# Storing the filter's spectrum during the weave of filter and first input, with e table 0 and fillers moved

## The chip, the cores and the metric

The kernel runs on one core of a Trainium2 chip: TensorE (PE, with its weight loads listed as PEld), VectorE (DVE), ScalarE (ACT), GpSimd (POOL) and SyncE (SP, which issues DMAs only). The metric is the device time of one execution in microseconds (us). Before the change the median of three runs is 2032.61 us (2030.9 to 2034.29).

## The reference

Two computations follow each other. The first is a long convolution of x (8 batches, 5696 positions, 128 channels) with a filter h, by Fourier transforms of length 11392; the second mixes its result over positions with two 5696x5696 matrices.

```python
Xf = np.fft.rfft(x, n=2 * S, axis=1)
Hf = np.fft.rfft(h, n=2 * S, axis=0)
y = np.fft.irfft(Xf * Hf[None], n=2 * S, axis=1)[:, :S]

theta = y @ w_theta
zr, zi = y * np.cos(theta), y * np.sin(theta)
m = einsum('ts,bsd->btd', w_tok_r, zr) + einsum('ts,bsd->btd', w_tok_i, zi)
u = y + m
out = u + np.maximum(u @ w_ch, 0.0)
```

## The kernel before

**Tiling of the convolution.** The transform of length 11392 is split into 178 x 64. The work is cut into eight groups, each two batches and one half (64) of the channels. A group has four stages. Stage A (`stage_a`, L242) multiplies by the first transform `f1_t`: 16 blocks of four matmuls, each block into one PSUM tile, which DVE (L258) or ACT (L260) copies into the tile `a`. The second transform (`f2`, L263) reads all of `a` and makes 12 blocks of 8 frequencies (the last has 2). In stage B (`stage_b`, L415) ACT copies each such block out of PSUM (`xs`, L435), and DVE multiplies it by the filter's spectrum into `uv_t` (L437 or, for group 0, L442). Stage C (`stage_c`, L448) needs all of `uv_t`: 16 blocks of 16 matmuls, copied out by DVE (L464) or ACT (L462) into `g`. Stage D multiplies by the `e` tables (`e_t`) and writes the result out. The program weaves the stages: stage C of a group with stage A of the next, then stage B of the next with stage D of the group.

**The filter first.** h goes through stage A and `f2` like an input. `h_chunk` (L360) does one block of its spectrum: `f2`, and a copy with a scale back into the place of h's own stage-A tile (`a_h`; a__240 in the profile), on DVE for five of the blocks (L365), on ACT for the others (L367). The 12 calls of `h_chunk` are woven with the 16 stage-A blocks of the first input x0 (`a0`, by the list `A_WITH`). This is called the weave here. Inside x0's blocks stand fillers, matmuls whose result nobody reads (`idle`, L237); the argument `spare` of `stage_a` says how many and how wide. The last third of the table `w_t2`, the small tables `r_u` and `r_v` and the start of `e` table 0 are made in the weave or right after it.

**Where the spectrum goes.** Group 0 takes it from `a_h` directly: the product needs the rows also swapped by 64, and for these two SP DMAs a block copy them into one of four `hs` tiles (L425). Four blocks' copies are issued by `load0`, and each block's step issues those of the fourth block after it. All later groups read the spectrum from HBM (`hf_hbm`, L427). Twelve SP DMAs store it there (`h_store`, L371 to L375), four for blocks 0 to 5, four for 6 to 10 and four for block 11; six more, from HBM to HBM, add the swapped rows (`swap_rows`, L405 to L410). Stage A of group 1 (`a__1406`) uses the buffer of `a_h`, so its first copy waits until all that reads `a_h` is done.

**What sets the order.** Up to the end of group 0's stage C, DVE, ACT and POOL run in the order in which the program is written (`manual_schedule`). PE and SP are ordered by a planner over the whole kernel, by priority and by its own estimates, with waits on semaphores; `issue_after` puts what stands in its block behind a given instruction on that instruction's engine. After group 0's stage C the planner orders all engines, apart from two stretches of the mixing in which DVE is fixed again.

**e tables.** `e_table(n)` (L393) gives four steps: the nearest whole turn (two DVE instructions, L399 and L400), the absolute value (DVE, L198), the sine (ACT, L195) and the cosine (ACT, L202), each over 90x979 elements. Tables 1 and 2 and the negatives (`e_minus`) are made in group 0's stage C. All three are first used in its stage D.

Of the kernel before, what the change touches and what calls it, by code (L numbers as in the profile page):

```python
# [22 lines left out]
def kernel(  # L23
# [10 lines left out]
    nc = tc.nc  # L34
# [44 lines left out]
    K1 = N1 // 2 + 1  # L79
# [8 lines left out]
    NCK = len(CHK)  # L88
# [15 lines left out]
    def psum():  # L104
        return fp.tile([P, 2, 512], F32, tag="ps", name="ps")
# [20 lines left out]
    a_0 = s1.tile([P, 2 * K1, HD], F16, name="a_0")  # L126
# [67 lines left out]
    def sine(out_, r, sign):  # L194
        nc.scalar.activation(out_, r, AF.Sin, bias=zero_b[:r.shape[0]], scale=-sign * TWO_PI)  # L195

    def absolute(k, r):
        nc.vector.tensor_scalar(k.bitcast(mybir.dt.uint32), r.bitcast(mybir.dt.uint32), 0x7FFFFFFF, None,  # L198
                                op0=ALU.bitwise_and)

    def cosine(out_, k):
        nc.scalar.activation(out_, k, AF.Sin, bias=half_pi[:k.shape[0]], scale=-TWO_PI)  # L202
# [6 lines left out]
    w_t2 = keep.tile([P, K1, 3 * N2], F16, tag="keep", name="w_t2")  # L209
# [27 lines left out]
    def idle(ps, n, of, m):  # L237

        for i in range(n):
            nc.tensor.matmul(ps[:, i % 2, 512 - m:], of[:, :P], of[:, P:P + m], start=True, stop=True)  # L240
# [83 lines left out]
    pad = v_t[:, 5 * D * CK:6 * D * CK]  # L324
# [20 lines left out]
    for n, f in enumerate(steps):  # L345
# [5 lines left out]
            w_rest(1)  # L351
        f()
    w2_absolute()

    def hst_of(c, n=1):
        c0 = CHK[c][0]
        c1 = CHK[c + n - 1][0] + CHK[c + n - 1][1]
        return a_h["a"].rearrange("p (h k) d -> p h (k d)", h=2)[:, :, c0 * HD:c1 * HD]

    def h_chunk(c):  # L360
        c0, ck = CHK[c]
        ps = f2(a_h, c, 0)
        dst = hst_of(c).rearrange("p h (d k) -> p h d k", k=ck)
        if c in (0, 2, 5, 7, 10):
            nc.vector.tensor_scalar(dst, ps, 16.0 / NF, None, op0=mult)  # L365
        else:
            nc.scalar.activation(dst, ps, AF.Copy, scale=16.0 / NF)  # L367
        for cc, j in ((0, 0), (NCK - 1, CHK[-1][1] - 1)):
            if c == cc:
                nc.vector.tensor_scalar(dst[:, :, :, j], dst[:, :, :, j], 0.5, None, op0=mult)  # L370
    def h_store(i):  # L371
        i, h, ri = i // 4, i // 2 % 2, i % 2
        c0, c1, w = ((0, NCK // 2, HD * CK), (NCK // 2, NCK - 1, HD * CK), (NCK - 1, NCK, HD * CHK[-1][1]))[i]
        nc.sync.dma_start(hf_hbm[c0:c1, h, :64, ri, :w].rearrange("c p n -> p c n"),
                          hst_of(c0, c1 - c0)[64 * ri:64 * ri + 64, h].rearrange("p (c n) -> p c n", n=w))  # L375
# [17 lines left out]
    def e_table(n):  # L393

        n0 = 11 * n
        t, k, r = ((e_y[0], e_f[1], e_y[0]), (e_y[1], e_y[0], e_y[1]), (e_f[2], e_y[1], e_y[0]))[n]

        def nearest():
            nc.vector.tensor_scalar(k, t, MAGIC, None, op0=add)  # L399
            nc.vector.scalar_tensor_tensor(r, k, MAGIC, t, op0=ALU.subtract, op1=ALU.subtract)  # L400
        t3, k3 = (z.rearrange("p (n m) -> p n m", m=NB) for z in (r, k))
        return (nearest, lambda: absolute(k, r), lambda: sine(e_t[:K1, n0:n0 + 11, 1, :], t3, -1),
                lambda: cosine(e_t[:K1, n0:n0 + 11, 0, :], k3))

    def swap_rows():  # L405
        for c0, c1, w in ((0, NCK // 2, HD * CK), (NCK // 2, NCK - 1, HD * CK), (NCK - 1, NCK, HD * CHK[-1][1])):
            for ri in range(2):
                dst, src = (hf_hbm[c0:c1, :, r0:r0 + 64, r, :w].rearrange("c h p n -> (c h) p n")
                            for r0, r in ((64, ri), (0, 1 - ri)))
                nc.sync.dma_start(dst, src)  # L410

    def e_minus():
        nc.vector.tensor_scalar(e_neg[:K1], e_t[:K1, 1:2 * NP:2], -1.0, None, op0=mult)

    def stage_b(a_st, dh, warm=WARM, first=False):  # L415

        hs_of = {}

        def load(c):
            if c >= NCK:  # L420
                return
            hs = hs_of[c] = fh.tile([P, 2, HD * CK], F16, tag="hs", name="hs")
            w = HD * CHK[c][1]
            for e in range(2 if first else 0):
                nc.sync.dma_start(hs[64 * e:64 * e + 64, 1, :w], hst_of(c)[64 - 64 * e:128 - 64 * e, dh])  # L425
            if not first:
                nc.sync.dma_start(hs[:, :, :w], hf_hbm[c, dh, :, :, :w])  # L427

        def chunk(c):
            c0, ck = CHK[c]  # L430
            hv = hs_of[c][:, :, :HD * ck].rearrange("p r (d k) -> p r d k", k=ck)
            straight = hst_of(c)[:, dh].rearrange("p (d k) -> p d k", k=ck).unsqueeze(1) if first else hv[:, 0:1]
            ps = f2(a_st, c, warm)
            xs = fs.tile([P, 2, HD, CK], F16, tag="xs", name="xs")
            nc.scalar.activation(xs[:, :, :, :ck], ps, AF.Copy)  # L435
            if ck == CK and not first:
                nc.vector.tensor_tensor(  # L437
                    uv[:, :, :, c0:c0 + ck],
                    xs.rearrange("p e d k -> p e (d k)").unsqueeze(1).to_broadcast([P, 2, 2, HD * CK]),
                    hv.rearrange("p r d k -> p r (d k)").unsqueeze(2).to_broadcast([P, 2, 2, HD * CK]), op=mult)  # L440
            for r in range(2 if ck < CK or first else 0):
                nc.vector.tensor_tensor(  # L442
                    uv[:, 2 * r:2 * r + 2, :, c0:c0 + ck], xs[:, :, :, :ck],
                    (hv[:, 1:2] if r else straight).to_broadcast([P, 2, HD, ck]), op=mult)
            load(c + LEAD)
        return [lambda c=c: load(c) for c in range(LEAD)], [lambda c=c: chunk(c) for c in range(NCK)]

    def stage_c(st, last):  # L448
# [65 lines left out]
    def front(g, by_dve=(), a_=None, spare=None):  # L514
        if g >= len(groups):
            return [], [], []
        bp, dh = groups[g]
        x16 = x16s[g].rearrange("p b n d -> p (b n) d")
        steps, a_st = stage_a(lambda q: x16[:NB, :, q], by_dve, a_, spare)
        return (steps, *stage_b(a_st, dh, 0 if g else WARM // 2, g == 0))  # L520

    A_WITH = (1, 1, 1, 2, 1, 2, 1, 2, 1, 2, 2)
    a0, load0, b0 = front(0, (1, 3, 5, 8, 11, 13), a_0, (1, w_t2[:, 2:5].rearrange("p k n -> p (k n)"), 512 - 4 * K1))
    rr = []
    r_rest = [lambda: rr.extend([r_table(0, r_u), r_table(1, r_v)]), lambda: rr[0](), lambda: rr[1]()]
    e0 = e_table(0)
    h_chunk(0)
    w2_sine()
    for c in range(1, NCK):
        if c == 5:  # L530
            w_rest(2)
        h_chunk(c)
        if c == 1:
            w2_cosine()
        for _ in range(min(len(a0), A_WITH[c - 1])):
            a0.pop(0)()
        if c in (8, 9, 10):
            r_rest.pop(0)()
    for f in load0:
        f()  # L540
    for f in e0[:2]:
        f()
    for f in a0:
        f()
    fronts = {1: front(1)}
    for n, f in enumerate(b0):
        f()
        h_store(n)
        if n in (3, 6):
            e0[n // 3 + 1]()  # L550
        if n % 2:
            idle(psum(), 1, w_t2[:, 2:6].rearrange("p k n -> p (k n)"), 512)
    idle(psum(), 6, w_t2[:, 2:6].rearrange("p k n -> p (k n)"), 512)
# [232 lines left out]
    for g, (bp, dh) in enumerate(groups):  # L786
        st = {}
        last = g + 1 == len(groups)
        a_, load_, b_ = fronts.pop(g + 1) if g + 1 in fronts else front(g + 1)
        if last:  # L790
            for _ in range(3):
                steps0.pop(0)()
        now = ([with_load(steps0.pop(0), n < 6) for n in range(9)] if last else [], 0.0, 0.88)
        c_ = stage_c(st, last)
        if g == 0:
            swap_rows()
            now = ([*e_table(1), *e_table(2), e_minus], -0.06, 0.62)
        woven((c_, 0.06 if a_ else 0.0, 1.0), (a_, 0.0, 0.88), now, load_, (load_x(g + 2, st), 0.1, 1.02))
        if g == 0:
            ordered.close()  # L800
        if g + 2 == len(groups):
            xin.close()
            open_phases()
            load_ya0()
        now = [steps0.pop(0) for _ in range(4)] if last else []
        woven((b_, 0.0, 0.8), (stage_d(st, bp, dh, load_ya1 if last else None, g + 2 == len(groups)), 0.08 if b_ else 0.0, 1.1 if b_ else 1.0), now)
        if g + 2 == len(groups):
            load_ya1(st["yt"], True)
            open_ring()
# [333 lines left out]
    for i, (k, p, tt, j0, s0, nj) in enumerate(stretches):  # L1143
# [47 lines left out]
        if tt is None:  # L1191
# [21 lines left out]
            if end_of_pair:  # L1213
# [5 lines left out]
                c, c0 = c_last  # L1219
# [183 lines left out]
```

## Time and profile before

| | |
|---|---|
| median of three runs | 2032.61 us |
| the profiled execution | 2031.42 us, span 2029.6 us |
| PE busy | 1944.0 us (96% of the span) |
| DVE, ACT, POOL busy | 1538.6, 636.1, 976.0 us |
| the weave: first matmul of h's second transform to the first of x0's | 25.09 to 47.84 us |
| group 0's product, up to the first long run of stage C | 47.84 to 67.16 us |
| group 0's stage C, up to its last copy | 67.16 to 93.4 us |
| group 1's stages A and C (for comparison) | 115.0 to 132.5 us |

A row of an engine's sequence shows the start, the time from there to the end of the last of the merged instructions, the engine, the line, the operation, what it writes and reads, the shape and the count; in brackets stands the engine's idle time before it and what ended it. A matmul's row includes its way through the array, so in a row of matmuls the distance of the starts tells the cost of one. A row of the table by stretches shows, for each engine, busy time and instructions, and at the end the clock that TensorE was granted (1.00 is full), a DMA share and the GB/s moved.

### The profile page before, as it was taken

What the parts mean: (1) busy time and instruction counts of PE and PEld (TensorE: products, weight loads), DVE (VectorE), ACT (ScalarE), POOL (GpSimd) and SP (SyncE); (2) the same over time, 40 slices, a digit from 0 to 9 for tenths busy, and PEclk for the clock granted to TensorE, in tenths of its full rate; (3) what the DMA queues carried; (4) which work ended last, traced back from release to release, by engine and by line L of the source; (5) the groups of instructions that cost most, each with busy time, mean ns of one, the idle gap of its engine ahead of it and who ended that gap; (6) DMA issues with size and microseconds to landing.
All of it is one profiled execution on the core that took longest, in us unless ns stands there. A gap on an engine that the chain in (4) does not pass through costs nothing.

```text
span 2029.6 us, 42459 instructions
## 1 busy us (share of the span) xinstructions
PE 1944.0 (96%) x16124; PEld 1077.7 (53%) x16300; DVE 1538.6 (76%) x2819; ACT 636.1 (31%) x934; POOL 976.0 (48%) x1787
## 2 busy tenths in 40 slices
PE   7789898889999999999999998999999999999998
PEld 6688888644444444444444444444444444444444
DVE  7777887766778787887877668768677776777767
ACT  6778887852232323232300000011111111111111
POOL 8333413584453635454566454554535445354450
PEclk8999999999999999999999999999999999999999
DMA  9999997999798989999999799896978879798793
GB/s 130 161 159 175 159 173 211 257 238 189 150 183 171 180 168 162 181 174 179 167 171 152 121 255 217 132 153 123 153 131 149 148 129 154 126 155 139 135 156 85
DMA packets 508525, 332.48 MB, mean 164 GB/s; under 512 B 186727, under 2 KB 461671, under 8 KB 508231
## 3 DMA queue, kind: packets, MB, share of 16 engines
q0 software_dynamic: 322656, 157.47, 61.1%
q1 hardware_dynamic: 177792, 159.17, 27.0%
q10 hardware_dynamic: 7872, 13.11, 1.9%
q8 instruction: 128, 2.10, 0.4%
q14 instruction: 77, 0.63, 0.1%
HBM read 373.24 MB, written 92.95 MB: 230 GB/s over the span
## 4 chain that ended last, share of the span: by engine, by line
PE 40%; DMA 4%; DVE 3%; POOL 2%; issue 2%; ACT 0%; DVEq 0%; POOLq 0%; ACTq 0%
PE m L1338 37%; POOL ring L687 2%; DMA ring<-in_moe_w_tok_i_dram 2%; DVE c L1345 1%; PE v L998 1%; PE utp L991 1%; PE m L1342 1%; DMA ring<-in_moe_w_tok_r_dram 1%; DVE wt L911 1%; DMA wl<-in_moe_w_tok_i_dram 0%; DVE b L848 0%; DMA cp_hbm<-c 0%; DMA wl<-in_moe_w_tok_r_dram 0%; PE m L1206 0%; DMA c<-cp_hbm 0%
## 5 line engine op out<-in xcount | busy, mean ns | idle before, releaser
L687 POOL DMA_DIRECT2D ring<-in_moe_w_tok_i_dram x720 | 388.7, 546 | 660.9 <-DVE wt L911 576.5
L911 DVE STREAM_TRANSPOSE wt<-ring 128x384 f32<-128x384 f32 (+2 forms) x720 | 359.6, 524 | 116.7 <-PE m L1338 74.9
L687 POOL DMA_DIRECT2D ring<-in_moe_w_tok_r_dram x720 | 387.3, 546 | 126.1 <-DVE wt L911 71.5
L1338 PE MATMUL m<-b,wt 128*128 128x512 bf16 x1600 | 382.7, 379 | 3.8 <-DVE wt L911 1.7
L1338 PEld LDWEIGHTS <-wt 128*128 128x128 bf16 x1804 | 176.0, 98 | 215.5 <-DVE wt L911 4.3
L1345 DVE TENSOR_TENSOR c<-c,m 128x512 f32<-128x512 f32 x412 | 266.1, 671 | 0.4 <-PE m L1338 0.4
L993 ACT ACTIVATE ring<-utp 128x512 bf16<-128x512 bf16 x85 | 50.7, 597 | 571.6 <-PE utp L991 571.6
L457 PE MATMUL ps<-r_u,uv_t 128*128 128x128 f16 x1024 | 118.8, 222 | 7.4 <-DVE g__1420 L464 3.7
L458 PE MATMUL ps<-r_v,uv_t 128*128 128x100 f16 x1024 | 116.8, 210 | 1.1 <-DVE uv_t L442 1.1
L988 ACT ACTIVATE ub<-c 128x512 bf16<-128x512 f32 x88 | 55.2, 628 | 199.3 <-DMA ring<-in_moe_w_tok_i_dram 116.9
L1239 PE MATMUL m<-b,wt 128*128 128x512 bf16 x471 | 111.4, 382 | 6.3 <-issue 3.0
L153 POOL DMA_DIRECT2D x<-in_x_dram x128 | 97.5, 767 | 23.8 <-POOL x L151 14.8
L458 PEld LDWEIGHTS <-uv_t 128*128 128x128 f16 x1024 | 101.5, 99 | 9.9 <-issue 7.4
L437 DVE TENSOR_TENSOR uv_t<-xs,hs 128x2048 f16<-128x2048 f16 x77 | 91.4, 1223 | 16.2 <-ACT xs L435 9.0
L457 PEld LDWEIGHTS <-uv_t 128*128 128x128 f16 x1024 | 101.6, 99 | 1.2 <-DVE uv_t L442 1.0
L435 ACT ACTIVATE xs<-ps 128x1024 f16<-128x1024 f32 x96 | 90.5, 972 | 25.9 <-PE ps L271 12.2
L1239 PEld LDWEIGHTS <-wt 128*128 128x128 bf16 x528 | 50.4, 98 | 64.7 <-issue 7.8
L573 ACT ACTIVATE red<-theta_ps,magic 128x512 f32<-128x512 f32 (+1 forms) x46 | 31.6, 687 | 153.5 <-PE theta_ps L571 96.3
L271 PEld LDWEIGHTS <-w_t 64*128 64x128 f16 x3240 | 57.9, 99 | 25.6 <-issue 20.7
L941 ACT ACTIVATE ring<-tpz 128x512 bf16<-128x512 bf16 (+1 forms) x46 | 27.5, 597 | 136.6 <-PE tpz L939 123.0
L251 PE MATMUL ps<-f_t,x 89*128 89x180 f16 x512 | 65.2, 258 | 1.9 <-DVE a__240 L365 1.1
L1000 DVE SCALAR_TENSOR_TENSOR c<-v,c 128x512 f32<-128x512 f32 x88 | 60.1, 684 | 2.8 <-PE v L998 2.1
(2932 smaller groups left out, 3737.2 us busy)
## 6 DMA issues: line engine op xcount, KB each, us to landing
ring<-in_moe_w_tok_r_dram POOLq DMA_DIRECT2D x352, 96.0 KB, 4.4
ring<-in_moe_w_tok_i_dram POOLq DMA_DIRECT2D x352, 96.0 KB, 4.9
ring<-in_moe_w_tok_r_dram POOLq DMA_DIRECT2D x352, 80.0 KB, 4.4
ring<-in_moe_w_tok_i_dram POOLq DMA_DIRECT2D x352, 80.0 KB, 3.9
cp_hbm<-c SPq DMA_DIRECT2D x88, 256.0 KB, 2.5
c<-cp_hbm SPq DMA_DIRECT2D x88, 256.0 KB, 4.3
out_dram<-c SPq DMA_DIRECT2D x88, 256.0 KB, 4.4
hs<-hf_hbm SPq DMA_DIRECT2D x77, 256.0 KB, 3.6
```

The source lines that it names most:

```text
L153: nc.gpsimd.dma_start(x16[p0:p1, e, n0:n0 + 16, :HD], bass.AP(tensor=src.tensor, offset=src.offset + (p0 * N2 + n0) * D + dh * HD, ap=[[N2 ...
L251: nc.tensor.matmul(ps[:, i // 2, (i % 2) * 2 * K1:(i % 2 + 1) * 2 * K1], lhs(q + i), f1_t[:NB], start=True, stop=True)
L435: nc.scalar.activation(xs[:, :, :, :ck], ps, AF.Copy)
L437: nc.vector.tensor_tensor(uv[:, :, :, c0:c0 + ck], xs.rearrange("p e d k -> p e (d k)").unsqueeze(1).to_broadcast([P, 2, 2, HD * CK]), hv. ...
L457: nc.tensor.matmul(o, u_t[:, at:at + P], r_u, start=True, stop=False)
L458: nc.tensor.matmul(o[:, 2 * NP:], v_t[:, at:at + P], r_v, start=False, stop=True)
L687: nc.gpsimd.dma_start(wb[32 * i:32 * i + 32, :ng, :nj * 64], bass.AP(tensor=a.tensor, offset=a.offset + row0 * S + p * H + i * QR + j0 * 6 ...
L911: nc.vector.transpose(wt.rearrange("p j t r -> p (j t r)").bitcast(F32).rearrange("p (j g t) -> p g j t", j=TJ, g=4)[:, :ng, :nj], wb[:, : ...
L1000: nc.vector.scalar_tensor_tensor(c[:m], v[:m], 0.0, c[:m], op0=ALU.max, op1=ALU.add)
L1239: nc.tensor.matmul(ms[n // 2 * 2 + h], a[n][:, j, :, r], bts_of[p][jj][n % 2 * 2 + h][:, r, :], start=(n % 2 == 0 and jj == 0 and r == 0), ...
L1338: nc.tensor.matmul(ms[q], a[q][:, j, :, r], bts[jj][q][:, r, :], start=(jj == 0 and r == 0), stop=(jj == NJ - 1 and r == 1 and q not in left))
L1345: nc.vector.tensor_tensor(c, z, ms[q], op=op)
```

## The change

Six things are edited, all ahead of the end of group 0's stage C.

1. Five fillers of 512 columns over the tile `pad` are put behind h's stage A and ahead of the first `h_chunk`.
2. The fillers inside x0's stage-A blocks go (one of 152 columns in each, now none).
3. Other blocks are given to DVE: of the spectrum 0, 2, 6, 8, 10 instead of 0, 2, 5, 7, 10; of x0's stage A 1, 3, 7, 9, 12, 14 instead of 1, 3, 5, 8, 11, 13.
4. The steps of the r tables follow blocks 9, 10 and 11 instead of 8, 9 and 10, and with them go the nearest turn, the absolute value and the sine of e table 0; its cosine follows the weave. Before, the DVE steps followed the weave, and the sine and the cosine followed blocks 3 and 6 of group 0's product.
5. The stores: four behind block 6 of the weave, four behind block 10, the last four behind block 0 of group 0's product. Before, one stood behind each of the product's twelve blocks.
6. The six DMAs of the swapped rows are put, on SP, behind the last copy into `hs` of group 0.

```diff
@@ -351,6 +351,7 @@
     w2_absolute()
+    idle(psum(), 5, pad, 512)
@@ -361,7 +362,7 @@
-        if c in (0, 2, 5, 7, 10):
+        if c in (0, 2, 6, 8, 10):
             nc.vector.tensor_scalar(dst, ps, 16.0 / NF, None, op0=mult)
@@ -412,6 +413,8 @@
+    last_hs = []
+
     def stage_b(a_st, dh, warm=WARM, first=False):
@@ -422,7 +425,7 @@
             for e in range(2 if first else 0):
-                nc.sync.dma_start(hs[64 * e:64 * e + 64, 1, :w], hst_of(c)[64 - 64 * e:128 - 64 * e, dh])
+                last_hs.append(nc.sync.dma_start(hs[64 * e:64 * e + 64, 1, :w], hst_of(c)[64 - 64 * e:128 - 64 * e, dh]))
@@ -520,10 +523,10 @@
-    a0, load0, b0 = front(0, (1, 3, 5, 8, 11, 13), a_0, (1, w_t2[:, 2:5].rearrange("p k n -> p (k n)"), 512 - 4 * K1))
+    a0, load0, b0 = front(0, (1, 3, 7, 9, 12, 14), a_0, (0, w_t2[:, 2:5].rearrange("p k n -> p (k n)"), 512 - 4 * K1))
...
-    e0 = e_table(0)
+    e0 = list(e_table(0))
@@ -534,20 +537,20 @@
         for _ in range(min(len(a0), A_WITH[c - 1])):
             a0.pop(0)()
-        if c in (8, 9, 10):
+        if c >= NCK - 3:
             r_rest.pop(0)()
-    for f in load0:
-        f()
-    for f in e0[:2]:
-        f()
-    for f in a0:
+            e0.pop(0)()
+        if c in (NCK // 2, NCK - 2):
+            for n in range(4):
+                h_store(n + (0 if c == NCK // 2 else 4))
+    for f in load0 + a0 + e0:
         f()
     fronts = {1: front(1)}
     for n, f in enumerate(b0):
         f()
-        h_store(n)
-        if n in (3, 6):
-            e0[n // 3 + 1]()
+        if n == 0:
+            for i in range(8, 12):
+                h_store(i)
@@ -793,7 +796,8 @@
         if g == 0:
-            swap_rows()
+            with tc.issue_after(last_hs[-1].ins):
+                swap_rows()
             now = ([*e_table(1), *e_table(2), e_minus], -0.06, 0.62)
```

## The prediction

> **What bounds the kernel now.** I read the page first (busy shares, the slices), then the stages by stretches of time, then each engine's own sequence of instructions at the two places that the change touches. From the page, the busy shares and the granted clock in 40 slices of about 51 us:
>
> ```profile
> PE 1944.0 (96%) x16124; PEld 1077.7 (53%) x16300; DVE 1538.6 (76%) x2819; ACT 636.1 (31%) x934; POOL 976.0 (48%) x1787
> PE   7789898889999999999999998999999999999998
> PEclk8999999999999999999999999999999999999999
> ```
>
> TensorE bounds the whole, but the first two slices are the emptiest, and the clock is below full in the first. All that is edited runs between 23 and 93 us; what comes later only starts earlier or later. Next the same stretch, cut where the granted clock changes (busy us of each engine, then clock, DMA share, GB/s):
>
> ```profile
> 21.97:25.38 3.41, 2.04 (x39) 1.84 (x39) 3.01 (x5) 3.41 (x6) 3.30 (x9) 1.00 1.13 68
> 25.38:28.79 3.41, 3.41 (x95) 2.97 (x88) 1.95 (x3) 2.56 (x4) 3.30 (x8) 0.50 0.02 5
> ...
> 32.20:35.62 3.42, 2.20 (x63) 1.96 (x55) 3.31 (x5) 2.60 (x4) 3.33 (x5) 1.00 1.61 160
> 35.62:39.03 3.41, 3.21 (x73) 2.59 (x72) 2.28 (x3) 0.77 (x1) 3.27 (x4) 0.50 1.94 209
> 39.03:42.44 3.41, 3.41 (x51) 2.80 (x52) 1.31 (x5) 3.40 (x6) 3.41 (x6) 0.50 1.40 215
> 42.44:45.86 3.42, 3.42 (x55) 2.98 (x55) 3.34 (x7) 1.57 (x3) 1.73 (x4) 0.50 2.40 145
> ...
> 66.30:69.73 3.43, 0.92 (x15) 0.81 (x16) 2.95 (x5) 0.00 (x0) 0.00 (x0) 1.00 0.59 113
> 69.73:73.15 3.42, 2.39 (x24) 2.38 (x24) 1.65 (x2) 2.57 (x4) 1.73 (x3) 0.50 0.54 157
> 73.15:76.56 3.41, 3.41 (x36) 3.41 (x35) 0.55 (x1) 3.41 (x5) 0.18 (x1) 0.50 1.04 282
> ```
>
> See that three stretches with a TensorE pause (2.04, 2.20 and 0.92 us busy) are each followed by half clock. After the second the clock stays at 0.50 up to 52.7 us, and there TensorE is full while DVE and ACT wait for it. Last, the sequences of PE, ACT, DVE and SP where group 0 passes from the product with the spectrum to stage C:
>
> ```profile
> 35.29 0.49 PE L251 MATMUL ps<-f_t,x 89*128 89x180 f16 x4 [1.14 <-DVE a__240 L365]
> ...
> 70.76 0.27 PE L457 MATMUL ps<-r_u,uv_t 128*128 128x128 f16 x1 [2.69 <-DVE g__1420 L464]
> ...
> 70.58 0.77 ACT L260 ACTIVATE a__1406<-ps 128x720 f16<-128x720 f32 x1 [6.13 <-DMA hf_hbm<-hf_hbm]
> ...
> 66.71 0.39 DVE L442 TENSOR_TENSOR uv_t<-xs,hs 128x256 f16<-128x256 f16 x1 [1.26 <-DMA hs<-a__240]
> ...
> 65.26 3.70 SPq L374 DMA_DIRECT2D hf_hbm<-a__240  x5
> 69.01 2.78 SPq L410 DMA_DIRECT2D hf_hbm<-hf_hbm  x3
> ```
>
> ACT stands still for 6.13 us. The row names the swap, but the tile that ACT is to write (a__1406) takes the place of the spectrum's tile (a__240), and what still reads a__240 then are the five stores of 65.26 to 68.96; with their fastest landing of 1.8 us the last ends at 70.2 to 70.7, where ACT starts. Meanwhile three PSUM buffers of four hold x1's stage-A blocks that ACT should empty, so TensorE pauses 2.69 us and falls to half clock.
>
> **The change part by part.** Three stretches carry it: the weave (25.09 to 47.84, 22.75 us), group 0's product (47.84 to 67.16, 19.3 us) and group 0's stage C (67.16 to 93.4, 26.2 us).
>
> *Fillers ahead of the weave.* Five 128x512 matmuls; seven such in a row at full clock take 1.80 us, so five about 1.2 us. TensorE idles 1.28 us before 25.09 (it waits for ACT's last copy of stage A), so they lie in that pause; late by the wait for a PSUM buffer they cost 0 to 0.3 us. They fill the stretch that preceded the first fall of the clock.
>
> *Fillers inside x0's stage A go.* Sixteen 128x152 matmuls, 0.13 us apart at half clock (45.92 to 46.05) and 0.07 at full: 1.1 to 2.1 us of TensorE, on the path where the clock is half.
>
> *DVE and ACT in the weave.* The change of who empties which block moves no total: 5 spectrum blocks and 6 stage-A blocks stay on DVE, 7 and 10 on ACT. e table 0 comes in: on DVE 0.66+1.17+0.67 = 2.5 us, on ACT 1.10+1.11 = 2.2 us. Needs then: DVE 5x1.22 + 6x0.90 + 0.85 (halved bins) + 1.68 (the last third of w) + 2.4 (r tables) + 0.64 + 2.5 = 19.6 us; ACT 6x1.02 + 0.38 + 10x0.77 + 2.87 (sines) + 2.2 = 19.3 us; TensorE at half clock 11.25x0.97 + 16x0.62 = 20.8 us, at full 11.25x0.58 + 16x0.37 = 12.4 us. So 22.75 us can shrink to about 19 (overlapping starts spare a little), a gain of 3.8; with the clock half all along and waits as now, 0.3. I take 2.3, nearer to the DVE and ACT sums, because one of the two long half-clock stretches should go.
>
> The rows say when the clock falls: after one pause of 1.14 us. The Trainium skill ("TensorE: Matmul & The Clock Gate", Part 1) says that free-running windows of 3413 ns decide; the trace agrees, its changes at 35.6, 52.7, 69.7 and 76.6 us lie on such a grid. The same page says to fear pauses over about 3 us and that one busy window restores full clock; the trace disagrees (1.14 us sufficed, and 39.03 to 45.86, busy throughout, stayed at 0.50). By that rule the weave would stay at full clock with or without fillers, the last rival below.
>
> *Group 0's product.* DVE is its chain: 22 products 0.605 us apart and two short ones, 13.9 us, after a lead-in of 2.1 us. It loses 0.61 us at 55.55 and 0.62 at 59.93 behind e table 0's sine and cosine on ACT, which now go before it; and 0.17 + 1.26 us for the copied halves (hs), whose last loads stood on SP behind a store (0.62 us at 62.79). All gone: 2.7 us. Against it: sine and cosine may stand before ACT's first copy; it has 1.13 us idle there, so up to 1.1 us is exposed, and four small stores (0.62 us each on SP) now follow the first block, ahead of the loads of block 5, which have some 0.8 us to spare. Ends 0.7 and 2.7; I take 1.8.
>
> *The stores.* Twelve DMAs of 0.57 to 1.10 us on SP. Eight now enter the queue in the weave; behind a store that waits for its spectrum blocks stand the first hs copies, which in the trace had all been issued by 34.1 us, ahead of any store. SP is nearly idle from 35 to 51, so I cost these at nothing; without that cover the first product would wait 2 to 3 us.
>
> *Stage C of group 0.* With the stores landed, a__240 is free when its last hs copy is read, about when the product ends, so ACT starts some 4 us sooner and the 2.69 us pause and the half clock of 69.7 to 76.6 go. There a block pair takes 2.12 us (72.24 to 74.36) against 1.14 (79.13 to 80.27), so three pairs lose about 3.1 us. What is late next are DVE and ACT: DVE 12x1.22 + 5.9 (e tables 1, 2 and the negatives) = 20.5 us, ACT 16x0.77 + 4x1.02 + 4x1.11 = 20.8 us. From 26.2 that leaves at most 5.2; lower end 1.5 (the clock falls anyway). I take 4.0.
>
> *Swapped rows.* Six DMAs, 13.8 us on SP from 69.01; they now follow the last hs copy, so they start at about 57 to 60 instead. Behind them wait group 1's loads (first at 82.89), which group 1's products already waited 0.35+2.13+0.47 us for. Both move forward by about the same; zero, between -1 and +1.
>
> Sum: 2.3 + 1.8 + 4.0 = 8.1 us, bounds 2.5 and 11.7. The profiled execution took 2031.42 us (span 2029.6 and 1.8 around it): 2023.3. The median of the runs is 1.2 above it, 2032.61: 2024.5, with 2020.9 and 2030.1 at the ends. From 93 us on nothing is edited, and TensorE is 96 to 99% busy from 500 us on, so a gain should reach the end.
>
> **The rivals.** *The clock falls in the weave all the same.* Full-clock TensorE waits for emptied buffers (12.4 us of work in 19) and has no fillers left; once down it stayed down for 17 us in the trace. Then 0.3 + 0.7 + 2.7 = 3.7: 2028.9. Against it: DVE's 1.7 us on w no longer keeps a spectrum block waiting (block 5 goes to ACT), which made the 1.14 us pause. The Trainium skill speaks for this rival: the same page, "A second HAM failure mode: psum-queue depth-cycling", has matmuls that wait on PSUM buffers make the clock oscillate. Chance 0.15.
>
> *The gain is given back in group 1.* If the swap is not earlier, its end stays at 82.8 while group 1's product begins 8 us sooner and waits that much longer for its rows: about 2032.5. For it: those 2.95 us of waits. Against it: SP reaches the swap once nothing but hs copies stands ahead. Chance 0.09.
>
> *Slower.* After group 0's stage C the order on every engine is the planner's, and a changed beginning can change it in groups 1 to 7. The trace has the price: at 109.09 TensorE comes out of a 2.31 us wait for ACT, then runs 110.7 to 117.5 at half clock (3.2 pairs, 3.1 us): 5.4 us an event. Two added events cancel the gain (2035.3), three make 2040.7. Against it: groups 1 to 6 have a settled rhythm of 36 to 37 us. Chance 0.14, most of it at three.
>
> *The clock never falls* up to stage C's end: the upper end, 11.7 us, 2020.9. Against it: DVE and ACT then need no wait at all. Chance 0.12.
>
> **How the numbers follow.** Forecast 2024.5 with 0.50. A measurement here tells about 0.2% (4.1 us) from no change. Faster by more: 0.48 of the forecast's 0.50, the last rival's 0.12, half of the first's 0.15: 0.67. Within: 0.02 + 0.08 + 0.09 + 0.02 = 0.21. Slower: 0.12. The range 2019.0 to 2034.5 takes in both bounds, the first, the second and the last rival; outside lie the slower one and a tail below.
>
> **What would show it.** Right: no store on SP after group 0's product and no ACT wait near 6 us before x1's first stage-A copy; group 0's product starting near 45.5 and stage C near 62, ending near 85; no 0.50 between 25.4 and 28.8 and none at stage C's start. Wrong: 0.50 through the weave; DVE waiting for hs in group 0; group 1's products waiting over 3 us for hs; new half-clock stretches in groups 1 to 7, or a conv part that ends where it ended.

## The result, and the profile after

The changed kernel takes 2041.74 us (median of 8 runs, 2037.25 to 2049.26), the kernel before 2032.82 us in as many (2029.51 to 2038.68). The ratio is 1.0047, with a 95% interval of 1.0027 to 1.0067: some 9 us slower, where 8 us faster was forecast. The profiled execution took 2043.13 us (span 2041.4).

First the page of the changed kernel: TensorE's busy time, its busy tenths and its granted clock in 40 slices of 51 us.

```profile
PE 1951.1 (96%) x16289; PEld 1074.5 (53%) x16289; DVE 1535.3 (75%) x2819; ACT 637.0 (31%) x934; POOL 977.6 (48%) x1787
...
PE   6789998899999999999999999999999999999998
...
PEclk8899899999999999999999999999999999999999
```

The first slice has lost a tenth of its busy time, and the second one a tenth of its clock. The stretches of the weave in the changed kernel (length, then busy us and instructions of PE, PEld, DVE, ACT and POOL, then clock, DMA share, GB/s) say where:

```profile
25.38:28.79 3.41, 2.95 (x129) 2.68 (x122) 2.90 (x4) 3.13 (x4) 3.30 (x7) 1.00 0.02 5
35.62:39.03 3.41, 0.31 (x4) 0.22 (x3) 0.00 (x0) 0.00 (x0) 3.27 (x4) 1.00 1.94 194
39.03:42.44 3.41, 0.00 (x0) 0.00 (x0) 0.00 (x0) 0.00 (x0) 3.41 (x6) 0.65 1.42 293
42.44:45.86 3.42, 0.00 (x0) 0.00 (x0) 0.00 (x0) 0.00 (x0) 2.02 (x5) 0.50 1.89 207
...
56.10:59.50 3.40, 0.00 (x0) 0.00 (x0) 0.00 (x0) 0.04 (x1) 0.00 (x0) 0.50 0.68 202
```

The weave begins as hoped, at full clock. Then TensorE, VectorE and ScalarE all stand still, twice, while the DMA engines move about 200 to 290 GB/s. What they wait for is in the sequences of ACT, DVE, PE and SP in the changed kernel; its lines are one to three further down than before (L366 and L368 copy a block of the spectrum, L375 stores it, L428 makes the copies into `hs`, L411 swaps the rows, L445 is the product):

```profile
46.13 1.02 ACT L368 ACTIVATE a__240<-ps 128x1024 f16<-128x1024 f32 x1 [11.77 <-DMA hf_hbm<-a__240]
59.46 0.38 ACT L368 ACTIVATE a__240<-ps 128x256 f16<-128x256 f32 x1 [6.61 <-DMA hf_hbm<-a__240]
78.72 1.43 ACT L260 ACTIVATE a__1396<-ps 128x720 f16<-128x720 f32 x2 [1.33 <-DMA hf_hbm<-hf_hbm]
...
46.15 1.22 DVE L366 TENSOR_SCALAR a__240<-ps 128x1024 f16<-128x1024 f32 x1 [11.32 <-DMA hf_hbm<-a__240]
74.94 0.69 DVE L445 TENSOR_TENSOR uv_t<-xs,hs 128x1024 f16<-128x1024 f16 x1 [0.94 <-DMA hs<-a__240]
...
47.21 0.76 PE L251 MATMUL ps<-f_t,x 89*128 89x180 f16 x4 [11.28 <-ACT a__240 L368]
60.97 1.89 PE L271 MATMUL ps<-a,w_t 64*128 64x64 f16 x64 [7.26 <-DVE a L258]
...
33.24 29.28 SPq L375 DMA_DIRECT2D hf_hbm<-a__240  x12
64.76 12.36 SPq L428 DMA_DIRECT2D hs<-a__240  x16
77.17 5.86 SPq L411 DMA_DIRECT2D hf_hbm<-hf_hbm  x4
```

The copies of *later* blocks of the spectrum into `a__240` wait for *stores of earlier* blocks out of it. The two waits of ACT and the one of DVE, which runs beside ACT's first, are these rows of the changed kernel's waits (total us, times, longest):

```profile
ACT a__240 L368 <- DMA hf_hbm<-a__240: 18.4, 2, 11.8
...
DVE a__240 L366 <- DMA hf_hbm<-a__240: 11.3, 1, 11.3
```

No byte is both read by the store and written by the copy. But the tile `a__240` holds a block in two halves (one of each 64 channels, L355), and one instruction copies both. As one span it runs from the block's columns in half 0 to those in half 1; between them lie half 1's columns of all earlier blocks. In the program's list of instructions exactly three copies carry waits on stores: those of blocks 7 and 8 on the two stores of half 1 of blocks 0 to 5, and that of block 11 on the two of half 1 of blocks 6 to 10. Half 0's stores, which lie below the span, hold nothing back.

In the kernel before, the planner had already put five stores on SP between 35.3 and 47.8 us, in the middle of the weave. They held nothing up, because in the written order every copy stood ahead of every store. So what the change moved is less the time of the stores than their place in the order by which waits are made.

The account, from the two profiled executions:

| stretch | before | after | gain |
|---|---|---|---|
| weave, to x0's second transform | 22.75 | 35.9 | -13.1 |
| group 0's product | 19.3 | 17.5 | 1.8 |
| group 0's stage C, to stage D's first matmul | 26.5 | 22.2 | 4.3 |
| sum: stage D's first matmul later by | | | -7.0 |
| from there to x2's first stage-A copy | 22.1 | 22.7 | -0.6 |
| groups 2 to 7, first stage-A copy to last | 198.6 | 202.0 | -3.4 |

The profiled span is 11.8 us longer; 11.0 of them are in this table.

### The profile page after: what moved, and what is told of

Same layout as the page of the kernel before. It is cut to its first block, busy times and chain, and to the rows that moved or that the text cites. A ratio compares the mean times of both kernels' runs of the same rounds, so it can differ in the third digit from the quotient of the medians.

```text
span 2041.4 us, 42616 instructions
## 1 busy us (share of the span) xinstructions
PE 1951.1 (96%) x16289; PEld 1074.5 (53%) x16289; DVE 1535.3 (75%) x2819; ACT 637.0 (31%) x934; POOL 977.6 (48%) x1787
## 4 chain that ended last, share of the span: by engine, by line
PE 40%; DMA 4%; DVE 3%; POOL 2%; issue 1%; ACT 0%; DVEq 0%; POOLq 0%; ACTq 0%
PE m L1342 37%; DMA ring<-in_moe_w_tok_i_dram 3%; POOL ring L690 2%; DVE c L1349 1%; PE v L1002 1%; PE utp L995 1%; PE m L1346 1%; DVE wt L915 0%; DVE b L852 0%; DMA wl<-in_moe_w_tok_i_dram 0%; DMA ring<-in_moe_w_tok_r_dram 0%; PE m L1210 0%; DMA wl<-in_moe_w_tok_r_dram 0%; POOL wl L962 0%; DVE c L1004 0%
## 5 line engine op out<-in xcount | busy, mean ns | idle before, releaser
L1342 PE MATMUL m<-b,wt 128*128 128x512 bf16 x1640 | 388.3, 379 | 1.9 <-DVE wt L915 1.7
L1243 PE MATMUL m<-b,wt 128*128 128x512 bf16 x480 | 113.7, 385 | 5.8 <-issue 2.3
```

Source lines behind the costliest of these rows:

```text
L1243: nc.tensor.matmul(ms[n // 2 * 2 + h], a[n][:, j, :, r], bts_of[p][jj][n % 2 * 2 + h][:, r, :], start=(n % 2 == 0 and jj == 0 and r == 0), ...
L1342: nc.tensor.matmul(ms[q], a[q][:, j, :, r], bts[jj][q][:, r, :], start=(jj == 0 and r == 0), stop=(jj == NJ - 1 and r == 1 and q not in left))
```

## The experiments

Unless said otherwise, each kernel is an edit of the changed kernel. The theory: the stores' early place makes the copies wait (the span). The rivals: another part of the change, or the stores' traffic as such.

**Half 1's stores behind the weave.**

```diff
-            for n in range(4):
+            for n in range(2):
                 h_store(n + (0 if c == NCK // 2 else 4))
+    for i in (2, 3, 6, 7):
+        h_store(i)
```

> The changed kernel with one thing moved: only the stores of the spectrum's half 0 stay in the weave, the four large ones of half 1 are issued behind its last block. Theory 1 (spanned write: a block's copy writes half 0 and half 1 in one instruction, its span from the one to the other covers the earlier blocks of half 1, so it waits until a store that reads them has landed): neither ACT nor DVE waits for a store in the weave, which takes 19 to 21 us instead of 35.9 (and 22.8 before); group 0's product and stage C stay at about 17.5 and 22 us as in the changed kernel; in all 2023 to 2027 us, 6 to 10 below the kernel before. Theory 2 (any store that reads the spectrum's tile holds back every later write to it): ACT still waits some 8 to 12 us behind block 6 for half 0's stores; 2033 to 2040. Theory 3 (the clock or the traffic, not the wait): the weave stays above 30 us.

Measured: 2031.74 us (12 runs), 0.9985 of before (0.9972 to 0.9997). No copy waits for a store any more; the weave takes 19.7 us, a gain of 3.0. The stall of the changed kernel is therefore worth 16.2 us (35.9 - 19.7), about its waits of 11.8 and 6.6. But the product, 17.5 us in the changed kernel, now takes 22. PE, DVE and SP in this kernel:

```profile
44.81 1.89 PE L271 MATMUL ps<-a,w_t 64*128 64x64 f16 x64 [3.85 <-DVE a L258]
...
55.50 0.69 DVE L445 TENSOR_TENSOR uv_t<-xs,hs 128x1024 f16<-128x1024 f16 x1 [2.93 <-DMA hs<-a__240]
59.21 0.69 DVE L445 TENSOR_TENSOR uv_t<-xs,hs 128x1024 f16<-128x1024 f16 x1 [2.42 <-DMA hs<-a__240]
...
33.26 16.34 SPq L375 DMA_DIRECT2D hf_hbm<-a__240  x8
49.70 2.44 SPq L428 DMA_DIRECT2D hs<-a__240  x2
52.19 3.13 SPq L375 DMA_DIRECT2D hf_hbm<-a__240  x4
```

DVE waits 5.3 us for the copies into `hs`. Two explanations: they stand behind stores on SP (the queue), or share the DMA engines with them (the traffic).

**The copies split by half, the stores as in the change.** This leaves every store where the change wrote it and takes only the span away.

```diff
-            nc.vector.tensor_scalar(dst, ps, 16.0 / NF, None, op0=mult)
+            nc.vector.tensor_scalar(dst[:, z], ps[:, z], 16.0 / NF, None, op0=mult)
```

(and so for ACT's copies and the halved bins, for z in 0 and 1.)

> The changed kernel with all stores where it has them, but each copy of a spectrum block split in two, one for each half, so that no write spans the other half's blocks. Theory 1: no wait for a store in the weave; 24 more instructions or so, each with its own fixed part (ACT 0.2, DVE 0.1 us, estimated from 0.38 us for 256 columns and 1.02 for 1024), 1 to 2 us more in the weave than with half 1's stores late: 21 to 23 us; in all 2024 to 2029. Theory 2: the waits of 11.8 and 6.6 us stay, 2040 or more. Theory 3: also 2040 or more.

Measured: 2030.81 us (12 runs), 0.9982 (0.9965 to 0.9998). No wait for a store, the weave 19.9 us. With the stores in their new place and the data the same, the stall is gone: the span is the cause. Again DVE waits for `hs` in the product (the rows of this kernel, with SP):

```profile
54.39 0.69 DVE L446 TENSOR_TENSOR uv_t<-xs,hs 128x1024 f16<-128x1024 f16 x1 [1.72 <-DMA hs<-a__240]
57.16 0.69 DVE L446 TENSOR_TENSOR uv_t<-xs,hs 128x1024 f16<-128x1024 f16 x1 [1.48 <-DMA hs<-a__240]
59.93 0.69 DVE L446 TENSOR_TENSOR uv_t<-xs,hs 128x1024 f16<-128x1024 f16 x1 [1.48 <-DMA hs<-a__240]
...
33.35 15.61 SPq L376 DMA_DIRECT2D hf_hbm<-a__240  x8
49.06 1.98 SPq L429 DMA_DIRECT2D hs<-a__240  x2
```

**The stores alone, in the kernel before.** Only these lines of the change, on the old kernel:

```diff
+        if c in (NCK // 2, NCK - 2):
+            for n in range(4):
+                h_store(n + (0 if c == NCK // 2 else 4))
...
-        h_store(n)
+        if n == 0:
+            for i in range(8, 12):
+                h_store(i)
```

> The kernel before with only the stores put into the weave as in the change (four behind block 6, four behind block 10, four behind block 0 of the product); fillers, e table 0, who copies what and the place of the swapped rows stay. Theory 1: ACT and DVE wait in the weave, at least as long as the two waits of the changed kernel (18.4 us on ACT) less what the slower weave hides; the weave 33 to 38 us; in all 2038 to 2048, so this part alone makes the change slower. If the loss came from the fillers, from e table 0 or from the changed division between ACT and DVE, this kernel would come out at 2033 or below, since the 6.1 us wait of ACT at stage C goes.

Measured: 2044.0 us (10 runs), 1.0044 (1.0031 to 1.0056). This part alone makes a kernel slower by as much as the whole change. ACT in this kernel, with both waits:

```profile
46.69 1.02 ACT L367 ACTIVATE a__240<-ps 128x1024 f16<-128x1024 f32 x1 [11.16 <-DMA hf_hbm<-a__240]
60.77 0.39 ACT L367 ACTIVATE a__240<-ps 128x256 f16<-128x256 f32 x1 [7.83 <-DMA hf_hbm<-a__240]
```

**Why the wait is so long: x1's loads held back.** Between 29 and 44 us GpSimd also issues the 16 loads of x1. Here they wait for x0's last stage-A block.

```diff
-    for n, f in enumerate(load_x(1)):
-        f()
...
+    for f in load_x(1, {"g": a_0[:, :1, 48:]}):
+        f()
```

> The changed kernel with the sixteen loads of x1 held back on POOL until x0's last stage-A block is copied, so that they do not share the DMA engines with the stores of the weave. If their traffic sets the length of the wait (stores land after 8.1 us in the median in the changed kernel, 4.4 in the kernel before), the first wait of 11.8 us falls to 6 to 8 us, the second (6.6 us, with little other traffic) stays at 5 to 7. If the stores themselves set it, the first stays near 11 to 12 us. The loads then end some 12 us after the weave, just ahead of x1's stage A; a total of 2034 to 2044 us tells little.

Measured, one execution: 2047.21 us (x1's own stage A is late by this edit, so the time says nothing). ACT's two waits in this kernel, whose tile is numbered 223:

```profile
43.44 1.02 ACT L365 ACTIVATE a__223<-ps 128x1024 f16<-128x1024 f32 x1 [9.12 <-DMA hf_hbm<-a__223]
56.80 0.38 ACT L365 ACTIVATE a__223<-ps 128x256 f16<-128x256 f32 x1 [6.66 <-DMA hf_hbm<-a__223]
```

The first falls by 2.7 us, and the landing of a 384 KB store from 8.1 to 5.7 us (4.4 in the kernel before); the second, where no load of x1 runs, stays. So x1's loads explain less than a quarter of the first wait; what is left is the stores' own issue and landing (in the changed kernel SP takes from 33.2 to 39.3 us for the first four, and a 384 KB store lands after some 8 us). Neither theory's number came out: the traffic beside the stores counts, but it isn't most of the wait.

**The queue or the traffic: all stores from GpSimd.** The twelve stores are issued by GpSimd, behind the weave; SP keeps the copies into `hs` alone.

```diff
-        nc.sync.dma_start(hf_hbm[c0:c1, h, :64, ri, :w].rearrange("c p n -> p c n"),
+        nc.gpsimd.dma_start(hf_hbm[c0:c1, h, :64, ri, :w].rearrange("c p n -> p c n"),
...
+    for i in range(12):
+        h_store(i)
```

> The changed kernel with all twelve stores issued by POOL behind the weave instead of by SP in it; the spectrum is complete by then, so no write can wait for a store, and SP has nothing but the hs copies. With half 1's stores late, group 0's product took 22 us instead of 17.5, DVE waiting 2.9 and 2.4 us for hs copies. Queue theory (the copies stood on SP behind stores): both waits go, the product takes 17.5 to 18.5 us, stage C starts at about 63 instead of 67, the total falls to 2025 to 2029, 5 to 8 below the kernel before. Traffic theory (the copies were issued in time but shared the DMA engines with the stores): the waits stay at 3 us or more, the total at 2030 to 2032.

Measured: 2030.81 us (12 runs), 0.9991 (0.9977 to 1.0004), not told from before. SP's one row up to 65 us, DVE's longest wait, and below them the stretch in which it falls, in this kernel:

```profile
27.98 37.25 SPq L428 DMA_DIRECT2D hs<-a__240  x24
...
57.79 0.69 DVE L445 TENSOR_TENSOR uv_t<-xs,hs 128x1024 f16<-128x1024 f16 x1 [5.25 <-DMA hs<-a__240]
```

```profile
52.68:56.10 3.42, 0.79 (x33) 0.62 (x33) 0.00 (x0) 0.34 (x1) 1.07 (x2) 1.00 0.99 305
```

Nothing stands ahead of the copies on SP, and DVE waits as long (6.3 us in all), at a DMA share of 0.99 and 305 GB/s. The queue theory falls. The twelve stores are 2.88 MB (4 x 384 + 4 x 320 + 4 x 16 KB), some 10 us at that rate, and the copies share it. (The share alone proves no full load: it is 1.94 in the changed kernel's stretch from 35.6 us.) The Trainium skill ("DMA: Bandwidth & Descriptors", "Issuing engines are not separate DMA queues") says that DMAs of all issuing engines end on the same 16 DMA engines and interleave there, so that another issuer saves only the issuing; the trace agrees, with the 5.25 us.

**The same, with the r tables' end and e table 0's absolute value (and with it the sine) behind the weave.** This shortens TensorE's pause ahead of the product (3.8 us), in which DVE's last stage-A block stands behind these steps.

```diff
-        if c >= NCK - 3:
+        if c == NCK - 3:
...
+    for f in r_rest + [e0.pop(0)]:
+        f()
```

> The same with the last steps of the r tables and the absolute value of e table 0 moved on DVE from inside the weave's last two blocks to behind it. With half 1's stores late TensorE idled 3.85 us ahead of the product because DVE copied the last but one stage-A block at 43.9 only, behind those steps, and the clock fell to half. If that is DVE's order, the product starts 1.5 to 2 us sooner and the pause falls to 2 us or less; the total 0.5 to 2 us below the run with POOL's stores. If the pause is worth nothing (the product is held up later anyway), the total is the same.

Measured: 2031.23 us, 0.9994 (0.9976 to 1.0011). The pause falls to 2.2 us and x0's second transform starts at 43.42 instead of 44.78, but group 0's last product starts at 66.5 instead of 67.2: what starts earlier waits for `hs` (5.6 us). Of 1.4 us, 0.7 are left; the copies set the end of the product more than its start does.

**GpSimd's stores on the kernel before.**

```diff
-        nc.sync.dma_start(hf_hbm[c0:c1, h, :64, ri, :w].rearrange("c p n -> p c n"),
+        nc.gpsimd.dma_start(hf_hbm[c0:c1, h, :64, ri, :w].rearrange("c p n -> p c n"),
...
+    for i in range(12):
+        h_store(i)
...
-        h_store(n)
```

> The kernel before with nothing changed but that POOL issues the twelve stores behind the weave. If the late stores on SP were all that stage C suffered from, ACT's wait of 6.1 us, TensorE's pause of 2.7 and the half clock at 69.7 go, and 3 to 5 us of the total: 2028 to 2031. The rest of the change (fillers, e table 0, who copies what) would then be worth the difference to the changed kernel with POOL's stores, 2 to 4 us. If the wait goes and the total stays within 1 us, stage C gives the gain back behind it.

Measured: 2032.33 us, 0.9998 (0.9984 to 1.0013). ACT's 6.1 us wait at stage C is gone, and DVE's wait for `hs` in the product rises from 1.4 to 4.3 us. Stage C gains nothing either: from the last product to x1's last copies it takes 23.0 us, 22.7 before. TensorE waits 2.35 and 1.31 us there for DVE's copies, and the clock is 0.50 behind these waits. The two other kernels with GpSimd's stores show the same (22.4 us), so their totals carry a loss that is not the product's; its cause is open.

**Without the five fillers** (of the kernel with half 1's stores behind the weave):

```diff
-    idle(psum(), 5, pad, 512)
```

> The kernel with half 1's stores late, without the five fillers ahead of the weave. If they keep the clock up, it shows 0.50 from 25.4 us on as the kernel before does, and the weave takes 1 to 3 us longer than 19.7. If the clock does not hang on them (no fillers at all are left in x0's stage A either), it stays at 1.00 there and the weave stays at 19.7. The total tells little in one look.

Measured, one execution: 2028.35 us. TensorE's pause before the weave is back, but the clock stays up and the weave takes 19.4 us, as the sequence of PE and the stretch behind the pause show:

```profile
25.06 1.11 PE L271 MATMUL ps<-a__240,w_t 64*128 64x64 f16 x64 [1.28 <-ACT a__240 L260]
```

```profile
25.38:28.79 3.41, 2.89 (x126) 2.62 (x119) 2.94 (x4) 3.12 (x4) 3.30 (x8) 1.00 0.02 5
```

**Where the stores cost least.** Four kernels with the copies split. Two write the later stores behind block 7 of the product: the four small ones alone, or the four of blocks 6 to 10 as well.

```diff
-        if n == 0:
+        if n == NCK - LEAD - 1:
             for i in range(8, 12):
                 h_store(i)
```

> Each half of a spectrum block copied by itself, stores 0 to 7 in the weave as in the change, the four small stores behind block 7 of group 0's product, after the last hs copies were issued. If the hs copies are late in the product because they stand behind stores on SP, DVE's waits for hs fall from 1.72+1.48+1.48 us (same kernel with the small stores behind block 0) to under 2 us in all, the product from about 21 to 18 us, and the median to about 2028. If it is the stores' traffic itself, the waits stay at 4 us or more (the small stores carry only 192 KB of 2.9 MB), the product at 20 us or more, and the median at 2030 to 2031.

> As the kernel before it in this call, but the four stores of blocks 6 to 10 (1.28 MB) also go behind block 7 of the product. If traffic makes the hs copies late, the first product finds an empty DMA system: hs waits under 1 us in all and a product of about 18 us, but x1's first stage-A copy waits for the late stores, 3 to 5 us at most (6.1 us before the change); median 2027 to 2031. If neither traffic nor the queue makes them late, hs waits of 4 us or more remain.

Measured: 2030.7 us, 0.9982 (0.9965 to 0.9999), and 2030.06 us, 0.9977 (0.9960 to 0.9994). SP's rows of the second kernel, and DVE's longest wait in it:

```profile
33.29 14.11 SPq L376 DMA_DIRECT2D hf_hbm<-a__240  x8
48.39 3.90 SPq L429 DMA_DIRECT2D hs<-a__240  x4
...
55.51 0.70 DVE L446 TENSOR_TENSOR uv_t<-xs,hs 128x1024 f16<-128x1024 f16 x1 [2.82 <-DMA hs<-a__240]
```

The second edit did not do what it says: the planner put all eight large stores at 33 to 47 us wherever they were written, so the two kernels differ little. The four small ones came singly between the copies, at 52 to 63 us, and not behind the last of them; they carry 64 KB, not 192. Both kernels answer the question of the small stores: with none of them ahead of the copies of 48 us, the waits are 5.0 and 4.1 us. So in the last two kernels the stores were pinned on SP behind the last copy into `hs`: stores 4 to 11, or all twelve.

```diff
+            with tc.issue_after(last_hs[-1].ins):
+                for i in range(4, 12):
+                    h_store(i)
```

> Each half of a spectrum block copied by itself; stores 0 to 3 in the weave as in the change; the other eight pinned on SP behind group 0's last hs copy (the kernel before this one only wrote them there, and the planner still put them at 33 to 48 us). If the stores' traffic makes the hs copies late, 1.34 MB less stands beside them: DVE's hs waits of 4.1 to 5.0 us fall under 1.5 us and the product from about 21 to 18 us; the price is that x1's first stage-A copy waits for the stores, which land by about 66 to 68 us, 3 to 6 us. Median 2028 to 2032. If the hs copies are late for another reason (the copies themselves, the loads of x1), the waits stay at 4 us.

> The same with all twelve stores behind the last hs copy: no store's traffic in the weave or the product at all. Traffic theory: hs waits under 0.5 us, the shortest product of all runs (16 to 17.5 us, start near 45, end near 62), then the longest wait of x1's first stage-A copy, 6 to 10 us for 2.9 MB at about 290 GB/s from 58 on; the gain of weave and product is spent there, median 2029 to 2034. Other reasons: hs waits of 3 us or more remain though no store runs.

Measured: 2033.46 us, 0.9989 (0.9978 to 1.0000), and 2041.09 us (6 runs), 1.0035 (1.0021 to 1.0048). DVE, ACT and SP in the kernel with all twelve behind:

```profile
58.03 0.69 DVE L446 TENSOR_TENSOR uv_t<-xs,hs 128x1024 f16<-128x1024 f16 x1 [0.18 <-DMA hs<-a__240]
...
76.01 1.43 ACT L260 ACTIVATE a__1410<-ps 128x720 f16<-128x720 f32 x2 [15.53 <-DMA hf_hbm<-hf_hbm]
...
59.84 14.50 SPq L376 DMA_DIRECT2D hf_hbm<-a__240  x12
```

and DVE and ACT in the one with eight behind:

```profile
55.11 0.69 DVE L446 TENSOR_TENSOR uv_t<-xs,hs 128x1024 f16<-128x1024 f16 x1 [0.86 <-DMA hs<-a__240]
58.73 0.69 DVE L446 TENSOR_TENSOR uv_t<-xs,hs 128x1024 f16<-128x1024 f16 x1 [1.07 <-DMA hs<-a__240]
...
73.82 1.43 ACT L260 ACTIVATE a__1410<-ps 128x720 f16<-128x720 f32 x2 [11.40 <-DMA hf_hbm<-a__240]
```

The waits for `hs` follow the stores' bytes beside them: in the variants of the changed kernel without a stall 4.1 us or more with eight large stores ahead of the product's end, 1.9 with four, 0.2 with none, and then it is 16.5 us to the last product. As GpSimd's kernel rules the queue out, the traffic is left. The price was forecast too low, 3 to 6 and 6 to 10 us: x1's first stage-A copy, which needs the tile, waits 11.4 and 15.5 us, because SP takes 14.5 us to issue the twelve stores (its row at 59.84; 7.9 us for the eight) before the last one's landing even begins.

Eight of the kernels, in us: the start of x0's second transform, the start of the last product of group 0 on DVE, that of x1's last stage-A copies on ACT, and the waits of DVE for `hs` and of ACT for `a_h`'s tile.

| kernel | product starts | last product | x1's last | `hs` waits | tile wait | ratio |
|---|---|---|---|---|---|---|
| before | 47.84 | 66.71 | 89.45 | 1.4 | 6.1 | 1 |
| after | 60.97 | 78.42 | 96.48 | 0.9 | 1.3 | 1.0047 |
| half 1 late | 44.81 | 66.27 | 84.32 | 5.3 | 0 | 0.9985 |
| copies split | 44.91 | 65.79 | 83.86 | 4.7 | 0 | 0.9982 |
| split, eight written late | 44.94 | 65.36 | 83.90 | 4.1 | 2.2 | 0.9977 |
| GpSimd | 44.78 | 67.22 | 89.58 | 6.3 | 0 | 0.9991 |
| eight pinned behind | 44.97 | 63.33 | 91.41 | 1.9 | 11.4 | 0.9989 |
| twelve pinned behind | 44.91 | 61.40 | 93.17 | 0.2 | 15.5 | 1.0035 |

Once the span is out of the way, only one of the places tried is told from the change's early one by its total: all twelve behind the copies is dearer by some 0.5%. The intervals of the others overlap. The three split kernels with the early place are faster than the kernel before by some 0.2%, with intervals that end just short of 1 (0.9994 to 0.9999).

## Why the prediction was wrong

**The step that failed is "The stores".** It cost the stores at nothing, with SP's idle time as their cover, and priced the loss of that cover at 2 to 3 us for the first product. (SP was not idle there either: five stores of the kernel before stand between 35.3 and 47.8 us.) It asked what is queued *behind* the stores on SP, and not who must wait until a store has *read* its tile. It used that very rule two lines on, for x1's stage A, which waits for `a__240`'s readers; but the spectrum's own later copies write the same tile, and in the change they come after the stores in the written order. Measured: 11.8 and 6.6 us of waits, 16.2 us of the weave.

**Fillers ahead of the weave, 0 to 0.3 us:** they cost nothing; the weave starts at 25.11 instead of 25.09 us.

**The weave, 2.3 us:** where no copy waits for a store, the gain is 2.9 to 3.0 us (half 1 late, copies split). The mechanism (DVE's and ACT's sums bound it, at full clock) and the size were right: with half 1 late DVE is busy 17.0 and ACT 17.3 of 19.7 us, and TensorE's last wait, 3.85 us, is for DVE. The changed kernel never showed it.

**Group 0's product, 1.8 us:** in the changed kernel 1.8, as forecast, but under a condition that the step did not name: the stall had let the stores land. So the hit was luck. Without the stall the product is 2 to 2.7 us *longer* than before, because the stores' 2.88 MB share the DMA engines with the copies into `hs`. The bounds 0.7 and 2.7 left a loss out, and they were too narrow. The kernel before had spread its stores: five up to 47.8 us, two in the product, and the last five behind it, at the price of ACT's 6.1 us.

**Stage C, 4.0 us:** 4.3. The 6.13 us wait fell to 1.3 us, as the step said, and the clock is 1.00 from 66.3 us on, through stage C's start. Without the stall (half 1 late, copies split) the gain is there too: from the last product to x1's last copies 18.1 us, 22.7 before. But the end of the wait alone doesn't bring it, as the kernels with GpSimd's stores show.

**Swapped rows, 0:** right within its bounds. In group 1, DVE waits 2.7 us for the stored rows, 3.0 before.

**The rivals.** "The clock falls in the weave all the same" is wrong: it is 1.00 from 25.4 us to the stall, through two waits for PSUM buffers (0.70 and 0.18 us), and in its variants without a stall at least to 39.0 us; there it falls between 41 and 45 us, in TensorE's pause of 2.2 to 4.0 us ahead of the product. The Trainium skill's rule behind that rival ("TensorE: Matmul & The Clock Gate", "A second HAM failure mode: psum-queue depth-cycling") is not borne out by these waits, but two of them are a weak test. "The gain is given back in group 1" is wrong, by the waits above. "Slower" had the sign but not the mechanism: 7.0 us of the loss are there at stage D's first matmul, ahead of anything that the planner could reorder in groups 2 to 7. Those took 3.4 us more in this profile, but 198.6 to 205.2 us over all profiles, with the longer ones in faster kernels too, so these 3.4 us are not put down to the change. "The clock never falls" could not come true behind a stall of 11 us.

**The expected 8 us without the stall** are not there either: x1's last copies come 5.1 to 5.6 us earlier (half 1 late, copies split), and the medians show 2 to 4 us. The product's loss explains the first difference: 3.0 in the weave, less 2.0 to 2.6 in the product, and 4.7 from the last product to x1's last copies. Why the medians give less than 5 is open; groups 2 to 7 vary from profile to profile by more than that.

## What to carry to other kernels

Moving a DMA that reads a tile up in the written order turns every later write to that tile into a possible waiter, even if the DMA's time on the queue hardly changes; list who writes the tile after it, and by what span the write is tracked, before costing the queue. A write in two strides counted here as a write of everything between them: split it, or keep the halves in tiles of their own. And a store taken off the path still carries its bytes: ask which small copy with a short due time shares the DMA engines with it, for here every place of 2.88 MB had its price, on whichever queue it stood.

## What the runs showed of the hardware

The clock's fall is not set by the length of a pause alone. A pause of 1.26 to 1.28 us before 25.07 us was followed by a clock of 0.50 or 0.55 in two profiles (before, and before with GpSimd's stores), and by 1.00 in two others: without the five fillers, shown above, and with the stores alone, whose instructions up to 33 us are those of the kernel before. PE and the stretch behind the pause in the kernel with the stores alone:

```profile
25.07 1.11 PE L271 MATMUL ps<-a__240,w_t 64*128 64x64 f16 x64 [1.26 <-ACT a__240 L260]
```

```profile
25.38:28.79 3.41, 3.04 (x129) 2.68 (x122) 2.93 (x4) 3.13 (x4) 3.30 (x8) 1.00 0.02 5
```

The clock changes on a grid of 3.41 us, as the prediction says, and the grid lies elsewhere in each profile. How much of its stretch on that grid TensorE was busy does not decide either: it was 2.04 us in the kernel before (21.97 to 25.38), 2.06 with GpSimd's stores on it (22.27 to 25.68) and 2.06 without the five fillers (22.45 to 25.86), and only the first two were followed by half clock.

So what the fillers are worth is open: with them the pause is 0.2 us and the clock was 1.00 in every profile, without them it went either way. And the landing of the same four 384 KB stores (the median) went from 4.4 us (before) to 8.1 (after), 5.7 with x1's loads held back, and 9.4 with the small stores late: how long a transfer takes to land depends on what runs beside it, and not on its size alone.
